# Starting x's sums one unit earlier, and completing the attention before them, in a fused attention, mixture-of-experts and gated-layer kernel

## The chip, the cores and the metric

The kernel runs on one core of a Trainium2 chip. The metric is device time in microseconds (us) of one execution. TensorE is called PE, VectorE DVE, ScalarE ACT, GpSimd POOL and SyncE SP, as in the profile.

## What is computed

Three layers follow one another on 2304 tokens of width 512. The attention is over blocks of 64 tokens and 8 heads; its output, with heads side by side, is the x of a mixture of four experts, and that layer's output is the x of a gated layer with root-mean-square normalization.

```python
scores = scale * np.matmul(q_c, k_c.transpose(0, 1, 2, 4, 3))
attn = np.exp(scores - np.max(scores, axis=-1, keepdims=True))
attn = attn / (np.sum(attn, axis=-1, keepdims=True) + 1e-09)
out = np.matmul(attn, v_c)                                   # blocks of 64
...
h = np.maximum(x @ w1[e], 0.0)                               # e = 0..3, 512 -> 1024
out += p[:, e:e + 1] * (h @ w2[e])
...
xn = x / rms * rms_g
g = xn @ w_gate                                              # 512 -> 1536
return (g / (1.0 + np.exp(-g)) * (xn @ w_val)) @ w_out
```

## The kernel before

The 2304 tokens are 18 tiles of 128 rows, worked in three **sets** of six tiles. A set is two blocks of three tiles, so a block is 384 tokens wide. The program runs the three sets through the experts first and then, in a second round, through the gated layer. One pass over a set consists of **units**: eight for the experts (two for each expert, numbered 0 to 7 here), three for the gated layer.

A unit of the experts has two halves. In the first, `hidden` (called twice, once for each of two pairs of feature tiles) makes the hidden values by a fast scheme of two-by-two block products: seven products of six matmuls each (line 709) in place of eight, so 14 **hidden products** in a unit. Their operands are not only x and the weights, but sums and differences of blocks of x and of the weights. Additions on DVE (the `u`, `v`, `d_ps` and `c_ps` of line 198) put the products together, ACT takes the rectified value (`hh`, line 799) and DVE its remainder (`hl`, line 802), since each number is held as a high and a low part. In the second half, `outer` multiplies the hidden values with the second weights: 72 **output products** (line 863), and DVE adds each tile to `acc` (line 1059).

**x's sums.** For each set the eight sums and differences of blocks of x are made by `x_sums` on DVE (lines 197 and 198 with `s` and `xr` in the rows), one instruction of 128x384 each. They lie in eight buffers of `tp`, a store of 32 buffers that also feeds the attention, the weight fetches and the decode. In the last unit's output products (`aside`) they are rounded into the operands `x` of the next set, and the eight buffers come free.

**The rest runs as chains beside the products.** `Chains` is a list of generators with a clock of its own, in planned microseconds. After each product `tick` moves the clock, and steps each chain that is due; `every` is the chain's spacing. So the order of instructions on every engine is fixed when the program is built. `force(c, until)` steps one chain without heed to the clock until a condition holds; meanwhile `rush` is set, pauses are skipped and no product is put between. The chains that matter here are:

- `attention(own(s + 1))`, the next set's attention, two tiles at a time: scores on PE (line 497), softmax on DVE, ACT and POOL (lines 577 to 604), transposes of the result (`trA`, line 521), a copy on ACT (`aT`, line 526), value matmuls (`pv`, line 544) and copies into `xr` (line 569). It is added in unit 1 of the first set and in unit 4 of the second;
- `decode`, which turns the gated layer's 64-bit weights into 32-bit floats by six DVE instructions (lines 401 to 415) and one on POOL, from the second set on. It needs three free buffers of `tp` more than `room[0]`, which is 8 in a pass's last two units, and stops while `hold[0]` is set, in the last unit;
- `prepare`, which splits the decoded weights (ACT line 231 and 443, POOL line 197) for storing;
- `norm(s - 1)`, added in unit 2 of the second and third set: six squares on ACT (line 891), a table load and a square root (line 895), and small DVE instructions (lines 894 to 904).

In a last unit that is not the final one the program sets `hold`, forces the next set's attention (or, later, its transposes) to completion, adds `x_sums` with a spacing of 0.8, and forces them to completion ahead of the output products.

Of the kernel before, what the change touches and what calls it, by code (L numbers as in the profile page):

```python
# [150 lines left out]
def fused_kernel(ctx, tc, qkv, probs, w12, wglu, gvec, out):  # L151
# [14 lines left out]
    NSET = 3  # L166
# [18 lines left out]
    work = Chains()  # L185
# [279 lines left out]
    def attention_tiles(u):  # L465
        return [[tp.get(f"{nm}{i}") for nm in ("qk_a", "qk_b", "v")] for i in u]
# [211 lines left out]
    def x_sums():  # L678
        while tp.free() < 9:
            yield  # L680
        for n in ORDER:
            yield from x_sum(n)
# [249 lines left out]
    with tc.manual_schedule():  # L932
        units = [[i, i + 1] for i in range(0, NTILE, 2)]
        own = lambda s: units[s * TPS // 2:(s + 1) * TPS // 2]
        make_identity(nc, ident)
        warm = sm.tile([P, 1], F32, tag="warm", name="warm")
        nc.vector.memset(warm, 0.0)
        nc.scalar.activation(warm, warm, AF.Exp)
        fetching = work.add(fetch())
        lead = [[i] for i in range(TPS)]  # L940
        tiles = [attention_tiles(u) for u in lead]
        for group in (range(TPB), range(TPB, len(lead))):
            for k in group:
                attention_dma(lead[k], tiles[k], (0, 1))
            work.step(fetching)
            for k in group:
                attention_dma(lead[k], tiles[k], (2,))
        nc.sync.dma_start(out=pr, in_=probs)
        for kd in range(KD):
            nc.sync.dma_start(out=gk[:, kd:kd + 1], in_=gvec[kd * P:(kd + 1) * P].rearrange("(p o) -> p o", o=1))  # L950
        ended = set()
        for n in (0, 1, 9, 3):
            x_tile_of(n)

        def unit(k):
            yield from attention_unit(lead[k], tiles[k], lambda: ended.add(k))

        def block(b):
            mine = range(TPB) if b == 0 else range(TPB, len(lead))
            while not all(k in ended for k in mine):  # L960
                yield {}, 1
            for fp in range(UF) if b == 0 else ():
                yield from plain(fp, 0, moe_use(fp), fp == UF - 1)

        scratch = banks.get("scratch")

        def idle(us):
            for _ in range(int(us / 0.15)):
                nc.tensor.transpose(scratch[:, :P], ident, ident)

        arrive = [3.5, 5.7, 7.6, 14.5, 16.0, 17.5]
        spared[0] = 5
        gen = work.race(
            [(unit(k), arrive[k], None) for k in range(len(lead))]
            + [(block(0), 10.0, None), (block(1), 20.0, None)],
            (weights(), 9.0, None, 0.2),
            idle,
        )
        spared[0] = 0
        banks.put(scratch)  # L980
        feeding = work.add(gen, 0.5)

        def x_rest():
            for n in (5, 4, 6):
                yield from x_sum(n)
                yield from x_parts(n, nc.vector, True)
            yield from x_sum(2)
            while not plain_done:
                yield
            yield from x_parts(2, nc.vector, True)  # L990
            x_done()

        for o in (4, 5, 6, 2):
            tmp[o] = [tp.get(f"s{o}_{k}") for k in range(KH)]
        for i in range(TPS):
            acc[i] = tp.get(f"acc_{i}")
        plain_done = []
        resting = work.add(x_rest(), 0.9)
        work.add(sums_of_first(), 1.6)
        nc.vector.tensor_reduce(psm, pr, axis=AX.X, op=ALU.add)  # L1000
        nc.vector.tensor_scalar_add(psm, psm, 1e-9)
        nc.vector.reciprocal(psm, psm)
        nc.vector.tensor_tensor(pr, pr, psm.to_broadcast([P, NTILE, E]), op=ALU.mult)

        for kind, s in [(kind, s) for kind in ("moe", "glu") for s in range(NSET)]:
            moe = kind == "moe"
            final = not moe and s == NSET - 1
            if moe:
                plan = [(e, [u * UF + k for k in range(UF)]) for e in range(E) for u in range(NF1 // 2 // UF)]
            else:  # L1010
                plan = [(0, [u * UF + k for k in range(UF)]) for u in range(NF2 // 2 // UF)]
            ahead = None
            for k, (e, fps) in enumerate(plan):
                end = k == len(plan) - 1
                if moe and (s, k) == (0, 1) and resting in work.chains:
                    work.force(resting, lambda: resting not in work.chains)
                room[0] = 6 if k == 0 else 8 if k >= len(plan) - 2 else 0
                if moe and (s, k) in ((0, 1), (1, 4)):
                    ahead = work.add(attention(own(s + 1)), first=True)
                if k == 2 and (s == 0) != moe:  # L1020
                    work.add(norm(s - 1 if moe else NSET - 1), 1.5)
                if moe and s == 0 and k == 1:
                    feeding[1] = feeding[3] = 0.8
                if moe and s == 1 and k == 0:
                    work.add(fetch64())
                    work.add(decode(), 1.15, busy=3.5)
                    work.add(prepare(), 1.0)
                if k == len(plan) - 2 and not final:
                    if ahead is None:
                        ahead = work.add(turn(0 if moe else s + 1), 1.0)  # L1030
                if end and not final:
                    hold[0] = True
                    if ahead in work.chains:
                        work.force(ahead, lambda: ahead not in work.chains)
                    summing = work.add(x_sums(), 0.8)
                for fp in fps:
                    if moe and (s, k) == (0, 0):
                        for _ in plain(fp, 1, moe_use(fp), fp == fps[-1]):
                            pass
                        if fp == fps[-1]:  # L1040
                            plain_done.append(True)
                    elif moe:
                        hidden((kind, s, e, fp), moe_use(fp))
                    else:
                        hidden((kind, s, -1, fp), gate_use(fp))
                        hidden((kind, s, -2, fp), val_use(fp))
                w2 = [weight(("w2", kind, s, e, 2 * fp + j)) for fp in fps for j in range(2)]
                if end and not final and summing in work.chains:
                    work.force(summing, lambda: summing not in work.chains)

                def flush(t, ps):
                    i = s * TPS + t
                    if moe:
                        if k == 0:
                            if i not in acc:
                                acc[i] = tp.get(f"acc_{i}")
                            nc.vector.tensor_scalar(acc[i], ps, pr[:, i, e:e + 1], None, op0=ALU.mult)
                        else:
                            nc.vector.scalar_tensor_tensor(  # L1059
                                out=acc[i], in0=ps, scalar=pr[:, i, e:e + 1], in1=acc[i],  # L1060
                                op0=ALU.mult, op1=ALU.add,
                            )
                        return
                    if k == 0:
                        acc["o", i] = tp.get(f"out_{i}")
                        nc.scalar.copy(acc["o", i], ps)
                    else:
                        add(nc.vector, acc["o", i], ps, acc["o", i])
                    if end:
                        o = acc.pop(("o", i))  # L1070
                        nc.sync.dma_start(out=out[i * P:(i + 1) * P, :], in_=o)
                        tp.put(o)

                def aside(n):
                    if end and not final and n < len(ORDER):
                        for _ in x_parts(ORDER[n], nc.gpsimd if n % 2 else nc.vector):
                            pass
                        if n == len(ORDER) - 1:
                            x_done()
                            hold[0] = False  # L1080

                outer(fps, w2, flush, aside)
        work.force(None, lambda: not work.chains)
# [59 lines left out]
```

## Time and profile before

| | us |
|---|---|
| median of 3 runs | 1230.82 (1230.81 to 1232.41) |
| the profiled execution | 1231.08 |
| its span, first to last instruction | 1229.3 |
| PE busy | 1212.4 |
| DVE busy | 786.6 |
| POOL busy | 543.0 |
| ACT busy | 447.1 |

The span is that of the instructions; 1.8 us of the profiled execution lie around it. Busy time says that an engine had work, not that it ran at its peak. The chain that ended last is followed back from the last instruction, at each step to what released it; PE holds 91% of it. In the rows below a group's time stands first as its start, then its length, both in us.

### The profile page before, as it was taken

How to read it: one execution, taken by the hardware profiler on the slowest of the kernel's cores; microseconds unless marked ns; L12 is line 12 of the kernel's file. 1: busy time of each engine (PE TensorE's matmuls, PEld its weight loads, DVE VectorE, ACT ScalarE, POOL GpSimd, SP SyncE). 2: the span in 40 equal slices, each digit the busy share in tenths (PEclk: the TensorE clock that was granted, in tenths of full speed). 3: DMA queues.
4: the chain of work that ended last, by engine and by line, in shares of the span. 5: the costliest groups of instructions: out<-in, count | busy, mean ns of one | idle time of the engine just before them, and what ended most of it. 6: DMA issues, size and time to landing. Idle time of an engine off the chain costs nothing.

```text
span 1229.3 us, 20740 instructions
## 1 busy us (share of the span) xinstructions
PE 1212.4 (99%) x7254; PEld 1106.1 (90%) x7254; DVE 786.6 (64%) x1396; ACT 447.1 (36%) x1062; POOL 543.0 (44%) x580
## 2 busy tenths in 40 slices
PE   8989999999999999999999999999999999999998
PEld 6889899989998988889999999999999999999997
DVE  5755544456788778686677765776766634763644
ACT  6444333333234243342244224333435241332211
POOL 4696666664363564436256454364314101131100
PEclk9999999999999999999999999999999999999999
DMA  8377455554578797656577577657866835855943
GB/s 297 120 264 281 164 197 188 190 190 177 182 264 274 243 328 263 232 172 244 208 237 279 199 255 237 200 166 263 304 211 238 302 117 197 290 192 189 302 136 126
DMA packets 140216, 274.06 MB, mean 223 GB/s; under 512 B 16208, under 2 KB 16208, under 8 KB 140112
## 3 DMA queue, kind: packets, MB, share of 16 engines
q1 hardware_dynamic: 140112, 272.73, 65.0%
q8 instruction: 58, 0.95, 0.3%
q14 instruction: 46, 0.38, 0.1%
HBM read 210.28 MB, written 62.39 MB: 222 GB/s over the span
## 4 chain that ended last, share of the span: by engine, by line
PE 91%; DVE 2%; POOL 2%; issue 2%; ACT 1%; DMA 1%; SPq 0%; POOLq 0%; DVEq 0%; ACTq 0%
PE o L863 42%; PE a_ps L709 13%; PE c_ps L709 13%; PE d_ps L709 13%; PE b_ps L709 7%; PE pv L544 1%; POOL w L197 1%; POOL tw L197 1%; PE xT L918 1%; PE sc L497 0%; DMA r<-in_w 0%; PE trA L521 0%; DVE d_ps L198 0%; DVE s L197 0%; DMA w1m<-w 0%
## 5 line engine op out<-in xcount | busy, mean ns | idle before, releaser
L863 PE MATMUL o<-w,hh 128*128 128x512 f32 x1584 | 489.7, 390 | 0.6 <-POOL w L197 0.6
L863 PEld LDWEIGHTS o<-w,hh 128*128 128x128 f32 x1584 | 296.0, 188 | 60.7 <-POOL w L197 1.4
L863 PE MATMUL o<-w,hl 128*128 128x512 f32 x792 | 308.4, 389 | 0.0
L197 POOL TENSOR_TENSOR w<-r,w 128x512 fp32r<-128x512 f32 (+1 forms) x146 | 163.6, 1130 | 165.7 <-ACT w L356 74.5
L709 PE MATMUL c_ps<-x,w 128*128 128x384 f32 x1080 | 216.9, 338 | 2.3 <-DVE d_ps L198 2.2
L709 PE MATMUL a_ps<-x,w 128*128 128x384 f32 x984 | 198.1, 337 | 1.4 <-ACT p L762 1.4
L709 PE MATMUL d_ps<-x,w 128*128 128x384 f32 x984 | 198.1, 337 | 0.0
L709 PEld LDWEIGHTS c_ps<-x,w 128*128 128x128 f32 x1080 | 188.4, 188 | 4.1 <-DVE d_ps L198 3.5
L197 POOL TENSOR_TENSOR hl<-silu,hh 128x384 fp32r<-128x384 f32 x54 | 54.8, 1027 | 287.2 <-ACT hh L836 217.9
L1059 DVE SCALAR_TENSOR_TENSOR acc<-o,pr,acc 128x512 f32<-128x512 f32 x126 | 94.2, 748 | 132.9 <-PE o L863 132.9
L709 PEld LDWEIGHTS a_ps<-x,w 128*128 128x128 f32 x984 | 172.9, 188 | 4.7 <-ACT p L762 2.0
L863 PEld LDWEIGHTS o<-w,hl 128*128 128x128 f32 x792 | 148.7, 188 | 31.0
L709 PEld LDWEIGHTS d_ps<-x,w 128*128 128x128 f32 x984 | 172.4, 188 | 0.1
L198 POOL TENSOR_TENSOR w<-w,sc 128x512 f32<-128x512 f32 x36 | 47.2, 1310 | 152.0 <-DVE sc L415 137.0
L198 DVE TENSOR_TENSOR u<-b_ps,p 128x384 f32<-128x384 f32 x82 | 45.6, 556 | 98.6 <-ACT p L762 52.4
L709 PE MATMUL b_ps<-x,w 128*128 128x384 f32 x492 | 99.1, 337 | 0.0
L762 ACT COPY p<-a_ps 128x384 f32<-128x384 f32 x82 | 39.4, 480 | 155.7 <-PE a_ps L709 155.5
L197 POOL TENSOR_TENSOR w<-tw,w 128x256 fp32r<-128x256 f32 x112 | 86.5, 781 | 16.9 <-ACT w L231 10.5
L799 ACT ACTIVATE hh<-d_ps 128x384 fp32r<-128x384 f32 x92 | 45.4, 493 | 121.0 <-DVE d_ps L198 121.0
L709 PEld LDWEIGHTS b_ps<-x,w 128*128 128x128 f32 x492 | 86.3, 188 | 0.1
L231 ACT CAST w<-tw 128x256 fp32r<-128x256 f32 x112 | 42.6, 406 | 95.4 <-POOL tw L197 93.1
L836 ACT CAST hh<-silu 128x384 fp32r<-128x384 f32 x72 | 35.9, 513 | 103.5 <-DVE silu L833 103.4
(110 smaller groups left out, 1346.8 us busy)
## 6 DMA issues: line engine op xcount, KB each, us to landing
w<-wgv SPq DMA_DIRECT2D x252, 256.0 KB, 3.9
w<-w1m SPq DMA_DIRECT2D x224, 256.0 KB, 5.2
r<-in_w SPq DMA_DIRECT2D x128, 256.0 KB, 4.8
w1m<-w SPq DMA_DIRECT2D x112, 256.0 KB, 2.5
wgv<-w SPq DMA_DIRECT2D x84, 256.0 KB, 4.8
raw<-in_wglu SPq DMA_DIRECT2D x36, 512.0 KB, 3.8
w<-wou SPq DMA_DIRECT2D x36, 512.0 KB, 7.7
wou<-q SPq DMA_DIRECT2D x24, 256.0 KB, 5.0
```

Of the source, the lines that this page charges most:

```text
L197: sub = lambda eng, o, a, b: eng.tensor_tensor(o, a, b, op=ALU.subtract)
L198: add = lambda eng, o, a, b: eng.tensor_tensor(o, a, b, op=ALU.add)
L231: nc.scalar.copy(halves(out[n])[:, 0], at[part_of[n]])
L544: nc.tensor.matmul(ps[n][lo:lo + CH, o:o + CH], vt[a][lo:lo + CH, hp, ch, :], aT[a][lo:lo + CH, q:q + CH], start=True, stop=True,)
L709: nc.tensor.matmul(ps[:, :NB], wv[:, wi, k, :], xs[n][:, xi, k, :], start=(first and k == 0 and m == 0), stop=(last and k == KH - 1 and m ...
L762: nc.scalar.copy(p1, v(a))
L799: nc.scalar.activation(hi, src, AF.Relu)
L836: nc.scalar.copy(hi, v)
L863: nc.tensor.matmul(ps, hs[fps[k], b, j][hx][:, r * P:(r + 1) * P], w2[2 * k + j][:, wi], start=((k, j, m) == (0, 0, 0)), stop=((k, j, m) = ...
L918: nc.tensor.transpose(ps[:, kd * P:(kd + 1) * P], a[:, kd * P:(kd + 1) * P], ident)
L1059: nc.vector.scalar_tensor_tensor(out=acc[i], in0=ps, scalar=pr[:, i, e:e + 1], in1=acc[i], op0=ALU.mult, op1=ALU.add,)
```

## The change

`x_sums` is added one unit earlier at the ends of the first and second set of the experts' pass, with a spacing of 1.8 in place of 0.8, and ahead of it the attention chain is forced to completion there if it is still in the list. The third set's end and those of the gated layer keep the sums in the last unit. Everything below moves by up to five lines (1059 becomes 1064).

```diff
-            ahead = None
+            ahead = summing = None
...
+                if k == len(plan) - 2 and moe and s + 1 < NSET:
+                    if ahead in work.chains:
+                        work.force(ahead, lambda: ahead not in work.chains)
+                    summing = work.add(x_sums(), 1.8)
                 if k == len(plan) - 2 and not final:
                     if ahead is None:
                         ahead = work.add(turn(0 if moe else s + 1), 1.0)
...
-                    summing = work.add(x_sums(), 0.8)
+                    if summing is None:
+                        summing = work.add(x_sums(), 0.8)
```

Three places show what this does to the order of instructions. In the rows a name's number is a buffer's, `x6` counts equal instructions, and `a_ps`, `b_ps`, `c_ps`, `d_ps` are PSUM banks.

The first is PE at the head of unit 6 of the second set, with that set's last pair of attention tiles. Before:

```order
L863 MATMUL o_6017<-w_5756,hl 128x512
L709 MATMUL a_ps<-x_3641,w_0_5784 128x384 x6
L497 MATMUL sc_6051<-qk_a_5961 64x64
...
L709 MATMUL b_ps<-x_3655,w_5_5803 128x384 x6
...
L709 MATMUL b_ps<-x_3655,w_5_5872 128x384 x6
L521 MATMUL trA_6217<-ident,at_6100 128x128 x4
L709 MATMUL d_ps<-x_3671,w_4_5889 128x384 x6
L521 MATMUL trA_6234<-ident,at_6101 128x128 x4
L709 MATMUL c_ps<-x_3687,w_6_5891 128x384 x6
L709 MATMUL a_ps<-x_3701,w_1_5904 128x384 x6
L544 MATMUL pv_6266<-aT_6222,v_5963 64x64
```

And now:

```order
L863 MATMUL o_6017<-w_5756,hl 128x512
L497 MATMUL sc_6049<-qk_a_5961 64x64
...
L497 MATMUL sc_6050<-qk_b_5965 64x64
L521 MATMUL trA_6110<-ident,at_6085 128x128 x4
L521 MATMUL trA_6117<-ident,at_6086 128x128 x4
L544 MATMUL pv_6124<-aT_6115,v_5963 64x64
...
L709 MATMUL a_ps<-x_3641,w_0_5784 128x384 x6
L709 MATMUL b_ps<-x_3655,w_5_5803 128x384 x6
```

The hidden products that stood ahead of the scores, between scores and transposes and ahead of the value matmuls now all stand behind the value matmuls.

The second is DVE around the second set's sums. Before, in the first half of unit 7's hidden products, with rows of a decode among them:

```order
L411 SCALAR_TENSOR_TENSOR w_6434<-sc,w_6434 128x512
L198 TENSOR_TENSOR s_0_6465<-xr 128x384
L413 TENSOR_SCALAR sc<-w_6434 128x512
L197 TENSOR_TENSOR s_0_6467<-s_0_6465,xr 128x384
L198 TENSOR_TENSOR u_6484<-b_ps,p_6470 128x384
L198 TENSOR_TENSOR s_1_6466<-xr 128x384
L198 TENSOR_TENSOR v_6497<-d_ps,u_6484 128x384
```

And now, in the second half of unit 6's hidden products and its output products:

```order
L198 TENSOR_TENSOR s_0_6300<-xr 128x384
L198 TENSOR_TENSOR d_ps<-d_ps,v_6289 128x384
L802 SCALAR_TENSOR_TENSOR hl<-a_ps,hh 128x384
L197 TENSOR_TENSOR s_0_6302<-s_0_6300,xr 128x384
L198 TENSOR_TENSOR c_ps<-c_ps,u_6276 128x384
...
L197 TENSOR_TENSOR s_1_6303<-s_1_6301,xr 128x384
L1064 SCALAR_TENSOR_TENSOR acc_3985<-o_6363,pr,acc_3985 128x512
L197 TENSOR_TENSOR s_0_6385<-xr 128x384
```

The sums stand a unit earlier and further apart, three of them ahead of the output products and five among them, and the decode's rows are gone from both places.

The third is DVE in unit 2 of the third set, where the norm of the second set's result runs. Before, in the output products:

```order
L409 TENSOR_SCALAR sc<-raw 128x512
L894 TENSOR_SCALAR ms<-ms 128x6
L1059 SCALAR_TENSOR_TENSOR acc_7032<-o_7667,pr,acc_7032 128x512
L411 SCALAR_TENSOR_TENSOR w_7628<-sc,w_7628 128x512
L413 TENSOR_SCALAR sc<-w_7628 128x512
L897 RECIPROCAL y<-y 128x6
L898 TENSOR_TENSOR z<-y 128x6
```

And now, in the second half of the hidden products:

```order
L894 TENSOR_SCALAR ms<-ms 128x6
L198 TENSOR_TENSOR u_7567<-b_ps,p_7548 128x384
L198 TENSOR_TENSOR v_7580<-d_ps,u_7567 128x384
L897 RECIPROCAL y<-y 128x6
L898 TENSOR_TENSOR z<-y 128x6
L198 TENSOR_TENSOR d_ps<-c_ps,v_7580 128x384
```

The norm's small steps moved from behind the hidden products to between their additions.

## Rows read from the trace of the kernel before

**Rows 1.** The page's line of busy times: engine, us, share of the span, instructions.

```profile
PE 1212.4 (99%) x7254; PEld 1106.1 (90%) x7254; DVE 786.6 (64%) x1396; ACT 447.1 (36%) x1062; POOL 543.0 (44%) x580
```

**Rows 2.** The chain that ended last: start us, length us, what.

```profile
248.36 16.33 PE o L863 x72
...
279.61 16.33 PE o L863 x72
...
310.50 16.33 PE o L863 x72
...
511.73 16.35 PE o L863 x72
...
544.92 16.33 PE o L863 x72
...
606.71 16.33 PE o L863 x72
...
637.60 16.33 PE o L863 x72
```

**Rows 3.** DVE's timeline (start, length, what) in unit 7 of the second set.

```profile
530.29 1.52 DVE L413 TENSOR_SCALAR sc<-w 128x512 uint32<-128x512 uint32 x1
```

**Rows 4.** The chain, then PE's timeline (idle before in brackets): unit 6, second set.

```profile
492.26 1.04 PE a_ps L709 x6
493.30 1.09 PE sc L497 x64
...
507.43 2.01 PE pv L544 x64
...
503.20 0.66 PE L521 MATMUL trA<-ident,at 128*128 128x128 f32 x4 [0.28 <-POOL at L604]
```

**Rows 5.** DVE's timeline: the softmax of the last pair of tiles, second set.

```profile
495.24 0.68 DVE L577 TENSOR_REDUCE mx<-sc 128x8 f32<-128x512 f32 x1
496.05 0.69 DVE L580 TENSOR_TENSOR e<-sc,mx 128x512 f32<-128x512 f32 x1
496.66 0.55 DVE L198 TENSOR_TENSOR u<-b_ps,p 128x384 f32<-128x384 f32 x1
...
501.14 0.67 DVE L599 TENSOR_REDUCE rs<-e 128x8 f32<-128x512 f32 x1
501.85 0.30 DVE L600 TENSOR_SCALAR rs<-rs 128x8 f32<-128x8 f32 x1
502.18 0.20 DVE L601 RECIPROCAL rs<-rs 128x8 f32<-128x8 f32 x1
```

**Rows 6.** ACT's timeline in unit 4 and POOL's in unit 6 of the second set.

```profile
450.45 1.07 ACT L526 COPY aT<-trA 128x512 f32<-128x512 f32 x2
...
502.53 1.19 POOL L604 TENSOR_TENSOR at<-e,rs 128x256 f32<-128x256 f32 x2 [0.41 <-DVE rs L601]
```

**Rows 7.** Stretches: length, five engines' busy us, PE's clock, DMA; then PE at the start.

```profile
1226.00:1227.00 1.00, 0.00 (x0) 0.00 (x0) 0.20 (x1) 0.00 (x0) 0.00 (x0) 1.00 0.00 0
...
1228.00:1229.30 1.30, 0.00 (x0) 0.00 (x0) 0.00 (x0) 0.00 (x0) 0.00 (x0) 0.50 0.00 0
...
3.52 0.71 PE L497 MATMUL sc<-qk_a 64*64 64x64 f32 x16 [3.52 <-DMA qk_a<-in_qkv]
...
4.80 1.33 PE L969 MATMUL scratch<-ident 128*128 128x128 f32 x5
...
7.12 0.90 PE L969 MATMUL scratch<-ident 128*128 128x128 f32 x3
...
9.02 1.94 PE L969 MATMUL scratch<-ident 128*128 128x128 f32 x15
```

**Rows 8.** The norm: DVE and PE in the second set's unit 2, ACT in the third's.

```profile
370.97 1.17 DVE L898 TENSOR_TENSOR z<-y 128x6 f32<-128x6 f32 x1
...
372.67 1.31 PE L709 MATMUL c_ps<-x,w 128*128 128x384 f32 x6 [1.39 <-DVE d_ps L198]
...
639.36 1.28 ACT L895 ACT_TABLE_LOAD   x1
```

## The prediction, made before the changed kernel ran

> **What bounds the kernel now.** I read the busy times first, then the chain of work that ended last in order of time, then each engine's timeline where the chain leaves TensorE. TensorE (PE) is busy 99% of the span, so only its waits can be won or lost [rows 1]. The chain gives a clock for every unit: from the start of one unit's 72 output products to the start of the next. An undisturbed unit takes 310.50 - 279.61 = 30.89 us [rows 2]: 16.33 of output products and 14 hidden products of 1.04. Compare the last units of the first two sets, where x's sums now stand. The first set's takes 279.61 - 248.36 = 31.25, so the sums cost 0.36. The second set's takes 544.92 - 511.73 = 33.19, so 2.30 [rows 2]. There the reader sees why: between the sums VectorE (DVE) also holds a half-finished decode, one of whose steps takes 1.52 us there [rows 3], and hidden products wait for banks that DVE has not drained. So 2.66 us in all can be won here.
>
> **The sums leave the last unit: -2.66.** Eight sums go to unit 6 in both sets. In the first set all eight stand among the hidden products of unit 6, 1.8 apart by the planner; in the second, three there and five among the output products, and the half decode is gone from unit 7. Both units 7 are then like the undisturbed one. I book the full 0.36 + 2.30. What hides the sums in unit 6 is DVE's slack there; if that cover fails, the nearest price is what the closely spaced eight cost in the first set, 0.36. For both sets that bounds the loss at 0.7, and the gain at 2.0 to 2.7.
>
> **The attention is forced a unit earlier: +8.2.** The new branch first completes the attention chain of the next set. In the first set that chain is long over. In the second it is not: its last pair of tiles begins in unit 6. Before, its score matmuls stand behind one hidden product, and eight hidden products run on PE before the first transpose, nine before the second, eleven before the value matmuls. Now all of that stands in one piece at the head of unit 6: scores, transposes, value matmuls, and only then the 14 products. PE takes its matmuls in order, so it waits for the whole softmax. The row of before shows that it does not step around such a wait: the transpose at 503.20 kept PE idle for 0.28 on GpSimd (POOL) although a hidden product stood behind it [rows 4].
>
> I walk the softmax from the rows of the same pair in before. The score matmuls begin at 492.3 in place of the product and end at 493.4, 1.04 earlier than now [rows 4]. That gains nothing, because the decode that DVE has queued ahead of the first maximum is unchanged: the maximum still starts at 495.24 [rows 5]. From there, with no product's work between: maximum to shift 0.81, shift to next maximum 0.61, again 0.81 and 0.61, so the first sum of exponentials starts at 498.08 (ScalarE's exponentials lie beside this). A sum is 0.71, the small addition 0.33, the reciprocal 0.20 [rows 5], 1.24 for each half: 500.56. POOL starts 0.15 later and its first tile is done after half of 1.19, with 0.07 to PE [rows 4, 6]: first transpose at 501.38. Second transpose 0.6 later, 0.66 long; the second copy of ScalarE half of 1.07 [rows 4, 6]; value matmuls at about 503.2. They take 2.01 [rows 4], and the 14 products 14 x 1.04 plus 0.2 of restart: the output products start at 519.97. Before they start at 511.73 [rows 2]. The step costs 8.2. The small additions take 0.3 to 0.6 each and POOL's queue or a buffer's store may add to that, so 7.5 to 9.2. ScalarE's and SP's queues move with it: the casts of this unit's output weights now stand behind the first product's copy, need POOL four times and are wanted 14 us later; the loads behind the block come from the slots that the products release, so they shift with PE and not against it.
>
> **What a silence of 8.0 us does to PE's clock: +2.2.** From 493.4 to 501.4 PE has nothing to do. Nowhere in before does it idle so long between its first and last matmul; the nearest rows are the ends of the trace. After PE's last matmul, with PE at 0.00, the granted clock is 1.00 from 1226 to 1227 and 0.50 in the last 1.3 us of the span [rows 7]. [...] The return is seen at the start: after 3.5 us of nothing, the filler transposes take 1.33/5 = 0.27 each from 4.80, 0.90/3 = 0.30 from 7.12 and 1.94/15 = 0.13 from 9.02 [rows 7]. (The granted clock prints 1.00 there; I take the durations.) So the slow stretch there ended between 7.96 and 9.02, 4.4 to 5.5 us after PE's first work at 3.52. If the return is as late here, half speed runs from 501.4 to somewhere between 505.8 and 508.7, the later end if it counts from the value matmuls. In it lie two transposes (+0.3 on the path), the value matmuls (2.01; +0.7 to +2.0) and 0.6 to 2.8 us of products at half speed (+0.3 to +1.4). Sum 1.3 to 3.7, and zero if the clock does not fall. I take 2.2.
>
> [...]
>
> **The decode is held off, and the third set's norm slides: +0.8.** From unit 6 on the eight buffers of the sums leave the decode too few, so it pauses for nearly two units and comes back later in the third set. It ends that set in the same place as before in DVE's order, so the later stage finds its weights. But buffers are now freer in unit 2 of the third set, and the norm's squares finish earlier. Before, the norm's small DVE steps stand among the output products there: the table load comes at 639.36 [rows 8], after the hidden products are over, and the unit takes 637.60 - 606.71 = 30.89 [rows 2], so it is free. Now they stand between a hidden product's additions, where the second set has them already, and there PE idled 1.39 behind one that took 1.17 [rows 8]. ScalarE has four casts less to do in the new place, worth some 0.6. I take 0.8 between 0 and 1.7.
>
> **How the numbers follow.** -2.7 + 8.2 + 2.2 + 0.8 = +8.5. The profiled execution is 1231.08 (span 1229.3, 1.8 around it), 0.26 above the median 1230.82 of the runs; on the median the forecast is 1239.3. The lows of the terms give -2.7 + 7.5 + 0 + 0 = +4.8 and the highs -2.0 + 9.2 + 3.7 + 1.7 = +12.6, but not all together: 1236.2 to 1242.8.
>
> **Rivals.**
> 1. The clock term is nil: the fall comes too late or the slow rate lies on matmuls that are bound by their issue. Then +6.3: 1237.1. For it: what resumes first are 64-wide matmuls, and no row isolates those at the low clock. Against: the 0.50 row. Chance 0.15.
> 2. Faster: PE passes the waiting transposes and runs products in the softmax's shadow, so that only the 2.66 remains: 1228.2. One mechanism, PE's order; it decides if the eight products of 8.3 us may run before the transposes. For it: weight loads overlap matmuls all through the trace. Against: the idle 0.28 at 503.20 with a product behind it. Chance 0.02.
> 3. No change: the softmax is much shorter than walked, since back to back each step meets an idle engine. It would have to take 2.7 us or so of PE's time, without the clock. Already the decode ahead of the maximum holds DVE until 495.24, 1.8 after the scores. Chance 0.03, near 1231.5.
> 4. Worse: the forced block also waits for a buffer whose store is still under way, or the held decode makes later products wait again. A transfer late by 4 us on one of the block's tiles gives +12.5: 1243.3. For it: the block takes its buffers at once instead of over a unit. Against: the same tiles get them at nearly the same point of the queues. Chance 0.08.
>
> The forecast has 0.72. Measurements of this kernel tell about 0.2% (2.5 us) from no change. Faster 0.02, within 0.2% 0.03, slower 0.95. The range 1236.0 to 1243.0 takes in rival 1 and most of the forecast's own spread, and leaves out rivals 2 and 3 and the most of 4.
>
> **What would show it.** In the profile of the changed kernel: PE idle some 8 us in one piece before a transpose in the second set's unit 6, released by POOL; the granted clock at 0.50 late in that piece and for a few us after it; that unit some 10 us longer up to its output products; both units 7 at 30.9; unit 2 of the third set between 30.9 and 32.6. If the transposes start within 3 us of the scores, or products stand before them, the step of +8.2 is wrong. If the second set's unit 7 keeps more than 1 us over 30.9, the gain is wrong.

## The result, and the profile after

| | before | after |
|---|---|---|
| median of 6 runs | 1230.88 (1230.75 to 1232.41) | 1239.28 (1238.63 to 1239.77) |
| ratio, 95% interval | | 1.0065 [1.0055, 1.0075] |
| the profiled execution | 1231.08 | 1239.62 |
| its span | 1229.3 | 1237.8 |

The change made the kernel slower by 8.4 us. The forecast was 1239.3. How the 8.5 us between the two spans came about is another matter, and two terms of the sum were not what they were taken for.

The page of after, line of busy times (answers to [rows 1]), and the longest of PE's waits in the whole trace (us in total, times, longest):

```profile
PE 1214.5 (98%) x7254; PEld 1108.4 (90%) x7254; DVE 787.9 (64%) x1397; ACT 446.3 (36%) x1061; POOL 542.6 (44%) x580
...
PE trA L521 <- POOL at L604: 9.7, 2, 7.8
```

PE's busy time grew by 2.1 us although it has the same 7254 instructions, and it now waits once for 7.8 us. That wait is the forced attention. PE's timeline of after in unit 6 of the second set shows it (start, length, what, idle before in brackets; answers to [rows 4]):

```profile
472.67 0.62 PE L863 MATMUL o<-w,hh 128*128 128x512 f32 x2
...
493.06 0.41 PE L497 MATMUL sc<-qk_b 64*64 64x64 f32 x16
501.24 1.97 PE L521 MATMUL trA<-ident,at 128*128 128x128 f32 x8 [7.77 <-POOL at L604]
...
503.89 2.67 PE L544 MATMUL pv<-aT,v 64*64 64x64 f32 x62 [0.27 <-ACT aT L526]
506.48 1.31 PE L709 MATMUL a_ps<-x,w 128*128 128x384 f32 x6
...
521.15 0.62 PE L863 MATMUL o<-w,hh 128*128 128x512 f32 x2
```

Scores, then nothing for 7.8 us, then transposes and value matmuls, and only then the first hidden product. The unit takes 521.15 - 472.67 = 48.48 from output products to output products, against 39.00 before. PE's clock is in the stretches of after (length, busy us of PE, its weight loads, DVE, ACT and POOL, granted clock, DMA; answers to [rows 7]):

```profile
497.00:498.00 1.00, 0.00 (x0) 0.00 (x0) 0.96 (x2) 0.51 (x1) 0.00 (x0) 1.00 0.84 328
498.00:499.00 1.00, 0.00 (x0) 0.00 (x0) 0.93 (x3) 0.63 (x1) 0.00 (x0) 0.70 0.34 135
...
504.00:505.00 1.00, 1.00 (x20) 1.00 (x22) 0.00 (x0) 0.14 (x1) 0.72 (x1) 0.50 0.00 0
505.00:506.00 1.00, 1.00 (x37) 1.00 (x36) 0.00 (x0) 0.00 (x0) 0.00 (x0) 0.89 0.02 8
```

The granted clock falls to 0.50 while PE is silent (0.70 in the us from 498) and is back between 505 and 506 (0.89 in that us). In the last us ahead of 505 PE gets through 20 small matmuls, in the next through 37. DVE is busy nearly all the time that PE waits (0.96, 0.93): the softmax is the bound there.

The units, each from the first output product of the unit before to its own (worked out from PE's timeline), tell where the 8.5 us lie. Rows with no difference over 0.1 us are left out.

| unit | before | after | difference |
|---|---|---|---|
| first set, unit 2 | 41.62 | 42.62 | +1.00 |
| first set, unit 7 | 31.25 | 30.90 | -0.35 |
| second set, unit 6 | 39.00 | 48.48 | +9.48 |
| second set, unit 7 | 33.19 | 30.89 | -2.30 |
| third set, unit 2 | 30.89 | 31.28 | +0.39 |
| third set, unit 7 | 30.89 | 31.85 | +0.96 |

That is +9.2; the stretch ahead of it gave back 0.5 and small rests 0.2. The +1.00 in the first set's unit 2 doesn't come from the change; it stands or is absent in kernels that are alike up to there, and the last section tells what it goes with. The chain that ended last, in after, shows the rest of the table (start, length; answers to [rows 2]). Its starts lie 0.16 behind those of the timeline, the differences agree:

```profile
521.31 16.33 PE o L863 x72
552.20 16.33 PE o L863 x72
...
613.99 16.33 PE o L863 x72
645.27 16.35 PE o L863 x72
...
771.50 16.35 PE o L863 x72
803.36 16.33 PE o L863 x72
```

The second set's unit 7 is at an undisturbed 552.20 - 521.31 = 30.89. The third set's units 2 and 7 are not: 645.27 - 613.99 = 31.28 and 803.36 - 771.50 = 31.86.

### The profile page after: what moved, and what is told of

Its sections match the earlier page's. It is cut to its first block, busy times and chain, and to the rows that moved or that the text cites. A ratio compares the mean times of both kernels' runs of the same rounds, so it can differ in the third digit from the quotient of the medians.

```text
span 1237.8 us, 20752 instructions
## 1 busy us (share of the span) xinstructions
PE 1214.5 (98%) x7254; PEld 1108.4 (90%) x7254; DVE 787.9 (64%) x1397; ACT 446.3 (36%) x1061; POOL 542.6 (44%) x580
## 4 chain that ended last, share of the span: by engine, by line
PE 58%; DVE 1%; issue 0%; ACT 0%; DVEq 0%; ACTq 0%
PE o L863 25%; PE c_ps L709 9%; PE a_ps L709 9%; PE d_ps L709 9%; PE b_ps L709 5%; PE xT L918 1%; PE pv L544 0%; PE trA L521 0%; DVE d_ps L198 0%; DVE u L198 0%; DVE s L197 0%; DVE acc L1064 0%; DVE z L898 0%; DVE v L198 0%; DVE out L198 0%
```

## Experiments

Edits are against after where nothing else is said. Each kernel was timed beside runs of the kernel before on the same chip.

### Which set the loss is in

The theory: all of it is in the second set, where the attention is not done yet. The rival: the sums themselves, put among a unit that is fuller, cost time in either set. One set at a time:

```diff
-                if k == len(plan) - 2 and moe and s + 1 < NSET:
+                if k == len(plan) - 2 and moe and s == 0:
```

> Only the first set's sums begin in unit 6; the second set's stay in unit 7. Theory (the forced attention of the second set is the cost): nothing is forced in the first set, its unit 7 goes from 31.25 to 30.89 us, and the whole is 0.3 to 0.5 below the kernel before, about 1230.5. Rival (the early sums themselves cost, by DVE work among unit 6's hidden products): the first set's unit 6 grows by 3 us or more and the whole stands near 1234.

Measured: 1231.20 (1230.51 to 1231.95) beside 1231.54, ratio 0.9997 [0.9988, 1.0007]. Unit 6 takes 30.89, so the eight sums cost nothing there; unit 7 takes 30.89 in place of 31.25. The gain of 0.36 is real in the rows and too small for the timed runs to tell.

```diff
+                if k == len(plan) - 2 and moe and s == 1:
```

> Only the second set's sums begin in unit 6, with the attention forced ahead of them. Theory: all the loss of the change is here, so 1239 to 1240, 0.4 above the full change; PE idle near 8 us in one piece in the second set's unit 6, that unit 9.5 longer, unit 7 at 30.9. Rival (the loss is shared by both sets): about 1235.

Measured: 1240.48 (1240.18 to 1241.66), ratio 1.0075 [1.0060, 1.0090]. The whole loss comes with the second set's sums. Unit 6 takes 49.45, unit 7 30.89, and the third set's 31.28 and 31.84 are there as in after.

### Force or sums

Only the force stays in unit 6; the sums go back to unit 7:

```diff
                     if ahead in work.chains:
                         work.force(ahead, lambda: ahead not in work.chains)
-                    summing = work.add(x_sums(), 1.8)
```

> The attention is forced at the head of unit 6, but x's sums stay in unit 7 with a spacing of 0.8. Theory: the forced block's 9.5 us (8.2 of softmax that nothing covers, 1.3 of slow clock) stay and the 2.66 of the sums is not won: 1240 to 1241.5. Rival (the sums' early place or the held decode makes the loss): near 1231.

Measured: 1241.52 (1240.71 to 1242.31), ratio 1.0080 [1.0063, 1.0096]. Unit 6 takes 49.79 without any sum in it, and the third set's units 2 and 7 are as before (30.89, 30.90). So the force alone makes the loss, and the two late losses come with the sums' new place.

Unit 7 takes 32.84, 1.95 more than an undisturbed one, and here no decode step stands among the sums: the last one ends at 542.30, the first sum starts at 546.94. DVE's timeline of two stretched sums and the addition that PE then waits for, 1.67:

```profile
549.84 1.57 DVE L198 TENSOR_TENSOR s<-xr 128x384 f32<-128x384 f32 x1
...
551.80 1.18 DVE L197 TENSOR_TENSOR s<-s,xr 128x384 f32<-128x384 f32 x1
...
554.31 0.55 DVE L198 TENSOR_TENSOR d_ps<-c_ps,v 128x384 f32<-128x384 f32 x1
```

POOL works on two tiles of 128x512 from 549.70 to 552.56. So closely spaced sums can cost nearly 2 us without any decode.

### The clock apart from the wait

55 transposes that nobody reads are put behind the scores of the last pair while the attention is forced. They do no work for the result; they keep PE from falling silent.

```diff
+        if work.rush and len(u) == 2:
+            fill = banks.get("fill")
+            for _ in range(55):
+                nc.tensor.transpose(fill[:, :P], ident, ident)
+            banks.put(fill)
```

> The changed kernel with 55 transposes of the identity into a spare bank between the scores and the transposes of the forced block, some 7 us of PE work that nobody reads; nothing else differs. Theory (part of the loss is the clock): granted clock 1.00 through the second set's unit 6, transposes and value matmuls back to 0.44 and 2.0 us, 1.3 us less than the full change: about 1238. Rival (the clock costs nothing): as the full change, 1239.3. If the filler delayed the softmax: above 1239.3.

Measured: 1238.67 (1238.05 to 1239.96), ratio 1.0060 [1.0045, 1.0075]. PE's timeline with the filler, same stretch, and the granted clock in it:

```profile
493.34 6.22 PE L502 MATMUL fill<-ident 128*128 128x128 f32 x55
501.19 1.23 PE L526 MATMUL trA<-ident,at 128*128 128x128 f32 x8 [1.62 <-POOL at L609]
...
503.09 2.08 PE L549 MATMUL pv<-aT,v 64*64 64x64 f32 x62 [0.25 <-ACT aT L531]
505.10 1.31 PE L714 MATMUL a_ps<-x,w 128*128 128x384 f32 x6
```

```profile
501.00:503.00 2.00, 1.55 (x10) 1.02 (x10) 0.00 (x0) 1.12 (x3) 1.40 (x3) 1.00 0.00 0
503.00:506.00 3.00, 2.91 (x67) 2.84 (x68) 0.69 (x1) 1.14 (x4) 0.73 (x1) 1.00 0.03 8
```

The first transpose still waits for POOL until 501.19, so the wait is the softmax's and not the clock's. With the clock at 1.00 the unit takes 47.16: 8.16 us over before. In after it took 48.48, so the clock cost 1.32, and it lies in two rows: the transposes took 1.97 in place of 1.23 and the value matmuls 2.67 in place of 2.08, 1.33 together. The first product takes 1.31 in both. The gain of the timed medians over after, 0.6 us, is inside their scatter; the rows carry this verdict.

The clock's price is not the same in each execution. With the force alone:

```profile
501.99 1.97 PE L521 MATMUL trA<-ident,at 128*128 128x128 f32 x8 [7.77 <-POOL at L604]
...
504.64 3.67 PE L544 MATMUL pv<-aT,v 64*64 64x64 f32 x62 [0.27 <-ACT aT L526]
508.24 1.63 PE L709 MATMUL a_ps<-x,w 128*128 128x384 f32 x6
```

```profile
507.81:508.81 1.00, 1.00 (x10) 0.88 (x7) 0.66 (x1) 0.46 (x1) 0.00 (x0) 0.50 0.00 0
508.81:509.81 1.00, 1.00 (x7) 1.00 (x6) 0.03 (x1) 0.43 (x2) 0.00 (x0) 0.93 0.00 0
```

The same silence of 7.77, but the clock is still at 0.50 up to 508.8, so all value matmuls (3.67, with the filler 2.08) and the first product (1.63, there 1.31) are slow: 49.79 - 47.16 = 2.63 for the clock. With the second set alone it was 49.45 - 47.16 = 2.29.

### The spacing of the sums

```diff
-                    summing = work.add(x_sums(), 1.8)
+                    summing = work.add(x_sums(), 0.8)
```

> The changed kernel with the sums' spacing back at 0.8. Theory (the spacing matters little where the sums have a unit of their own): the first set's unit 6 0 to 0.4 longer, the second set's unit 6 within 0.4 of the full change apart from the clock's own scatter of some 1.3, in all 1239 to 1241.

Measured: 1240.34 (1239.86 to 1240.56), ratio 1.0072 [1.0057, 1.0087]. The first set's unit 6 takes 31.25 and its unit 7 30.89: close together, the sums cost 0.36 in either of the first set's two places. The second set's unit 6 takes 49.21, which is within the clock's scatter. So in the first set the wider spacing is worth 0.36 us. Other places have other prices: 1.95 with the force alone, nothing in the next run.

### Are the 2.30 us the sums or the half decode?

The prediction booked 2.30 in the second set's unit 7 to the sums leaving, and the half decode with them. In before, that unit held both. Here the sums stay in unit 7 and only the decode is held off a unit earlier. This edit is against before:

```diff
+                if moe and (s, k) == (1, 6):
+                    hold[0] = True
```

> The kernel before, with the decode held from the second set's unit 6 on in place of unit 7; the sums stay in unit 7. Theory: the held decode alone makes the third set's unit 2 (30.89 to 31.3) and unit 7 (30.89 to 31.85) longer, +1.35, and since no half decode is left in the second set's unit 7, that falls from 33.2 to about 31.25, -1.95: in all -0.6. Rival (what lengthens the third set is the shift of the attention or the sums): third set's units at 30.89, in all -1.95.

Measured: 1235.14 (1234.85 to 1236.55), ratio 1.0034 [1.0021, 1.0047]; the expectation was wrong in sign. But unit 7 of the second set takes 30.89 with all eight closely spaced sums in it. So in before the 2.30 need the half decode: without it the same sums are free. It is not the decode as such, for with the force alone the sums cost 1.95 in that unit without any. The rest was a surprise: the third set's unit 7 takes 33.31 (before 30.89), and in the gated layer two units take 46.02 and 48.86 (before 45.54 and 45.45): 2.42 + 0.48 + 3.41 = +6.3. Here is that unit 7, DVE's timeline, POOL's, and PE's wait:

```profile
789.93 1.57 DVE L197 TENSOR_TENSOR s<-xr 128x384 f32<-128x384 f32 x1
...
791.89 1.18 DVE L197 TENSOR_TENSOR s<-xr 128x384 f32<-128x384 f32 x1
```

```profile
789.79 2.86 POOL L197 TENSOR_TENSOR w<-r,w 128x512 fp32r<-128x512 f32 x2 [2.53 <-DMA w<-wgv]
```

```profile
795.00 1.31 PE L709 MATMUL c_ps<-x,w 128*128 128x384 f32 x6 [2.14 <-DVE d_ps L198]
```

Two sums that take 0.55 elsewhere take 1.57 and 1.18 while POOL works on its tiles of 128x512, the additions of the products behind them are late, and PE waits 2.14.

### Two ways to spare the wait

The forced block waits because the attention is not done in unit 6. First way: start it a unit earlier.

```diff
-                if moe and (s, k) in ((0, 1), (1, 4)):
+                if moe and (s, k) in ((0, 1), (1, 3)):
```

> The changed kernel with one number more: the second set's attention is started in unit 3 in place of unit 4, so that it ends of itself before unit 6 and nothing is left to force. Theory (the forced block is the loss; the rest of the change wins 2.66 and loses 1.35 by the held decode): no idle time of PE over 2 us in the second set, unit 6 at 30.9, unit 7 at 30.9, third set's unit 2 at 31.3 and unit 7 at 31.85, in all 1.3 below the kernel before. Rival (the wide sums lose by themselves): above the kernel before.

Measured: 1246.20 (1244.97 to 1246.88), ratio 1.0119 [1.0104, 1.0134]. A plain miss: 14.7 us slower. Unit 6 is indeed at 30.90, so the force finds nothing left. But units 4 and 5 take 42.84 and 41.44 (before 32.19 and 35.65): units 3 to 7 sum to 178.27 against 170.93, +7.3. PE's timeline of that kernel:

```profile
412.71 0.66 PE L521 MATMUL trA<-ident,at 128*128 128x128 f32 x4 [1.95 <-POOL at L604]
...
445.94 0.66 PE L521 MATMUL trA<-ident,at 128*128 128x128 f32 x4 [2.13 <-POOL at L604]
```

The attention's price moves with it, and transposes wait about 2 us at a time (7.4 in four waits over the trace, 1.9 in two before). Of the rest 6.4 lie in the third set (31.59 and 32.78 in units 2 and 7) and in the gated layer (45.88 and 48.88), much as with the held decode.

Second way: leave the attention alone, and let the sums wait for it.

```diff
+    def x_sums_behind(c):
+        while c in work.chains:
+            yield
+        yield from x_sums()
...
-                    if ahead in work.chains:
-                        work.force(ahead, lambda: ahead not in work.chains)
-                    summing = work.add(x_sums(), 1.8)
+                    summing = work.add(x_sums_behind(ahead), 1.8)
```

> The changed kernel without its force: x's sums are added in unit 6, but they wait until the attention has ended by its own pace. Theory: unit 6 of the second set back to 39.0, as before; the sums begin among its output products and end in unit 7, so of that unit's 2.30 a part stays (0.4 to 1.5); the decode is hardly held, so the third set is as before. In all 1 to 2 below the kernel before.

Measured: 1229.25 (1229.05 to 1229.68) beside 1231.45, ratio 0.9981 [0.9971, 0.9991]: faster than both kernels. Its chain in the second set's units 6 and 7:

```profile
507.51 2.01 PE pv L544 x64
...
511.81 16.35 PE o L868 x72
...
528.93 0.34 DVE sc L409
...
530.39 1.50 DVE sc L413
...
543.56 16.33 PE o L868 x72
```

No forced block: the value matmuls come at 507.51 behind their products, as in [rows 4], and unit 6 keeps its 39.01. Unit 7 takes 543.56 - 511.81 = 31.75. The half decode is still among its sums (528.93 to 531.89, once more with a step of 1.50 as in [rows 3]), but the sums are spaced wider. So 1.44 of the 2.30 are won, the first set's 0.36 besides, and the third set is as before. These 1.80 are the gain that the rows show; the other 0.4 between the medians lie within the spread of the runs of before (1230.91 to 1232.64).

Last, the same with the second set's sums at 0.8; this edit is against the variant just shown:

```diff
-                    summing = work.add(x_sums_behind(ahead), 1.8)
+                    summing = work.add(x_sums_behind(ahead), 1.8 if s == 0 else 0.8)
```

> The variant without the force, with the second set's sums 0.8 apart. Now all eight end before unit 7's hidden products, but they take their buffers before the decode starts its next word, which so is put off as in the changed kernel. Theory (a put-off decode is paid for later, and how much hangs on where its steps fall): unit 7 of the second set 30.9 to 31.2 in place of 31.75, and 0.4 to 6 more in the third set and the first units of the gated layer, so above the variant with 1.8. Rival (putting off one word is free): 0.7 below that variant.

Measured: 1235.65 (1234.72 to 1236.50), ratio 1.0031 [1.0019, 1.0044]. The second set's units are at 38.99 and 30.89, so the full 2.30 is there; but the third set's unit 7 takes 33.31 and two gated units 46.00 and 48.88, the price that the held decode paid.

That price goes with the order of the instructions. The decode has 36 words, each of them the six DVE instructions once. Counted in the built order, so many are done ahead of the sums of each end:

| kernel | second set's end | third set's end | first gated set's end |
|---|---|---|---|
| before, sums behind the attention | 15 to 16 | 31 | 36 |
| after | 15 | 31 | 36 |
| second set alone | 15 | 31 | 36 |
| force alone | 17 | 31 | 36 |
| held decode, attention earlier, sums behind it at 0.8 | 15 | 29 | 35 |

A word put off in unit 7 of the second set is made up by the end of the third, as in after, for 0.39 + 0.96, or it isn't, and then costs 6.3. The table shows that the two go together, not how a late word leads to the waits. Why after makes it up and the held decode doesn't was not tried: the force shifts the planner's clock, and that is the suspect.

## Why the prediction was right, and where it wasn't

**The sums leave the last unit, -2.66: right in size, its reason left open.** The rows give -0.35 and -2.30. The first set's part is the sums' close spacing, as said. For the second set's part the prediction saw the decode's 1.52 step among the sums [rows 3] and booked the gain to both of them going. With the decode held off and the sums left in unit 7, the unit takes the same 30.89, so it was enough that the decode went; no run has the decode there without the sums. But with the force alone the sums cost 1.95 in that unit without a decode. What the stretched DVE rows have in common, decode step or sum, is a POOL tile of 128x512 beside them (in before the 1.52 at 530.29 meets one that runs from 530.21 to 531.53). That this meeting makes the loss is read from the rows; no run took the tiles away. That a unit's cost goes when the sums go doesn't tell which of their neighbours made it.

**The attention forced a unit earlier, +8.2: right.** With the clock kept up the unit lost 8.16. The walk put the first transpose at 501.38; it came at 501.24. After reaches this unit 0.11 later than before does (472.67 and 472.56), so on the walk's own clock that is 501.13. Step by step, DVE's timeline of after (answers to [rows 5]):

```profile
495.34 0.68 DVE L577 TENSOR_REDUCE mx<-sc 128x8 f32<-128x512 f32 x1
...
498.08 0.68 DVE L599 TENSOR_REDUCE rs<-e 128x8 f32<-128x512 f32 x1
...
500.11 0.20 DVE L601 RECIPROCAL rs<-rs 128x8 f32<-128x8 f32 x1
```

Less the 0.11, the maximum starts at 495.23 (walk 495.24): the earlier scores did not move it. The first sum of exponentials starts at 497.97, 0.11 ahead of the walk (that 498.08 stands in both is chance), and the last reciprocal ends at 500.20, 0.36 ahead of it. A chain walked from the same operations' rows in another place held, because nothing else was queued on DVE between them.

**PE's clock, +2.2: it fell, to 0.50, but cost 1.32 here.** The step that failed is the return, which was read from durations at the start of before, where the granted clock prints 1.00. The prediction let some products run at half speed (0.3 to 1.4); in after the clock was back before the first product, and only transposes and value matmuls paid, 0.74 and 0.59. The transposes were put at 0.3, less than half of that, and the value matmuls at 0.7 to 2.0. In other executions of the same block it cost 2.05 to 2.63. So 2.2 was a fair middle and 1.32 the low end of what was given; the term is no constant.

**Decode and norm, +0.8: 0.39 and 0.96.** The norm's part (0 to 1.7, 0.8 taken) was 0.39. After's chain there, with the norm's `z` between a product's additions:

```profile
642.68 0.75 DVE z L898
643.43 0.49 DVE d_ps L198
...
643.96 1.31 PE c_ps L709 x6
```

The `z` takes 0.75 there, and not the 1.17 of [rows 8]. PE's last product starts at 643.96, 1.32 behind the one before it (642.64) where 1.04 is usual, so the wait itself is 0.28 of the 0.39. What the prediction excluded, "it ends that set in the same place as before in DVE's order", is true but for one place, and that place cost 0.96. In the third set's unit 7 the last decode's final step now stands just ahead of the sums. DVE's timeline of after, then POOL's:

```profile
788.54 0.68 DVE L415 SCALAR_TENSOR_TENSOR sc<-raw,sc 128x512 f32<-128x512 uint32 x1
789.14 0.55 DVE L198 TENSOR_TENSOR s<-xr 128x384 f32<-128x384 f32 x1
789.79 1.47 DVE L197 TENSOR_TENSOR s<-s,xr 128x384 f32<-128x384 f32 x1
...
791.65 1.18 DVE L198 TENSOR_TENSOR s<-xr 128x384 f32<-128x384 f32 x1
```

```profile
789.37 1.48 POOL L198 TENSOR_TENSOR w<-w,sc 128x512 f32<-128x512 f32 x1 [6.38 <-DVE sc L415]
790.81 1.60 POOL L197 TENSOR_TENSOR w<-r,w 128x512 fp32r<-128x512 f32 x1
```

POOL is released by that decode (bracket) and runs its two tiles beside the sums. Two sums of 0.55 take 1.47 and 1.18, and PE waits 0.69 for an addition behind them; before, one took 1.20 and PE waited for none. This unit is not in [rows 2], since the change does not touch it.

The sum by the rows is -2.65 + 8.16 + 1.32 + 1.35 = +8.2, and the spans give +8.5. The errors of two terms, -0.9 and +0.55, nearly cancelled, and the first set's unit 2 and the start added +0.5, less 0.2 of small rests. That the median came within 0.1 us of the forecast is therefore luck; that the attention's wait makes nearly all of the loss is not.

**The rivals.** The clock term is not nil, 1.32 to 2.63 (1). That no row isolates 64-wide matmuls at the low clock was a misreading, if the durations at the start are taken as the prediction takes them: 16 scores take 0.71 at 3.52 [rows 7], and 0.41 at 493.06 above. The granted clock prints 1.00 at both; for value matmuls, 64 wide too, after shows it: 20 in the us at 0.50, 37 in the one at 0.89. PE does not pass the waiting transposes (2): it ran nothing in 7.77 us though products stood behind, and with the filler it took the work in its order too. The softmax is as long as walked (3). No transfer held the block up (4): the waits in it are for POOL and for ACT alone.

## What to carry to other kernels

To force a chain to its end is to put its latency on the engine that all wait for (8.16 us here): walk the chain from its own rows elsewhere in the trace, and add the clock's loss as a range (1.32 to 2.63 here), not as a number. Here the consumer could wait for the chain by itself, and that was 10 us better than the force. Before you book a gain to the step that leaves a place, ask which of its neighbours there was the cause; and where DVE's rows stretch beside POOL's (1.47 in place of 0.55 here), a shift by one instruction far behind the change can go with the loss of a microsecond (0.96 here).

## What the runs showed of the hardware

**Some DVE instructions lasted until a POOL instruction beside them had ended (1.04 and 1.75 in place of 0.30), or past it (1.47 in place of 0.55).** The first set's unit 2, counted from the output products of unit 1, takes 41.6 or 41.7 us in six of the eleven profiled executions and 42.4 to 42.6 in the other five. It goes with one DVE row at the start of that stretch, 1.75 long in those five and 1.04 to 1.06 in the six; in after, and in before:

```profile
79.14 1.75 DVE L600 TENSOR_SCALAR rs<-rs 128x8 f32<-128x8 f32 x1
```

```profile
79.63 1.04 DVE L600 TENSOR_SCALAR rs<-rs 128x8 f32<-128x8 f32 x1
```

POOL's timeline beside it, of after and of before:

```profile
78.86 1.31 POOL L197 TENSOR_TENSOR w<-r,w 128x512 fp32r<-128x512 f32 x1
80.11 0.76 POOL L197 TENSOR_TENSOR w<-tw,w 128x256 fp32r<-128x256 f32 x1
```

```profile
79.36 1.28 POOL L197 TENSOR_TENSOR w<-r,w 128x512 fp32r<-128x512 f32 x1
```

Eight numbers per row, 0.30 us in [rows 5], take 1.75 or 1.04. In before the instruction ends with the POOL instruction that it met (80.67 and 80.64), in after only with the one behind that (80.89 and 80.87). What decides between the two was not tried; kernels that are alike there fall on either side. The third set's stretched sum ends 0.41 behind POOL's first tile (789.79 + 1.47 = 791.26, and 789.37 + 1.48 = 790.85). Not every DVE instruction is stretched: in before the `hl` at 78.46 takes its usual 0.55 beside POOL tiles that run from 77.41 to 79.41. What sets these apart no run shows.

**The clock's return after the same silence varies.** The silence was 7.77 us each time; full speed was back within 505 to 506 us in one execution (first transpose at 501.24) and only about 508.8 in another (first transpose at 501.99). No run here tells what decides it.
